# Linear attention and a sine-gated MLP in one kernel: the left-over token groups move into tile 1, batch 2 is held back, and one cast changes engine

## The chip, the cores and the metric

The kernel runs on one NeuronCore of a Trainium2 chip. The metric is the device time of one execution in microseconds. Three runs of the kernel before took 285.49, 285.60 and 286.18 us: the median is 285.6 us. The execution that was profiled took 285.96 us.

The engines are named as the profile names them: PE is TensorE (matmuls into PSUM), PEld its weight loads, DVE is VectorE, ACT is ScalarE, POOL is GpSimd and SP is the engine that issues most DMAs. Each works through its own queue in order; an instruction that waits holds up everything behind it on that engine.

## The reference

For q, k and v of shape (8 batches, 8 heads, 576 tokens, 64):

```python
q_s = softmax(q, over the 64 features)
k_s = softmax(k, over the 576 tokens)
kv  = einsum('bhsd,bhse->bhde', k_s, v)
x   = einsum('bhsd,bhde->bhse', q_s, kv)      # -> (4608 tokens, 512)
h   = x @ w_in                                # (4608, 2048)
g   = h + sin(alpha * h)**2 / (alpha + 1e-9)
out = g @ w_out                               # (4608, 512), float32
```

The two large products, x @ w_in and g @ w_out, are most of the arithmetic. The kernel computes in bf16 with float32 accumulation.

## The kernel before

**Tokens.** The 576 tokens of a batch are nine groups (j = 0 to 8) of 64. The MLP works on nine tiles of 512 tokens. Tile 0 is groups 0 to 7 of batch 0 and tile 1 is groups 0 to 7 of batch 1, so that the MLP can start when one batch is half prepared. The ninth groups of batches 0 and 1, 128 tokens together, are the first two groups of tile 2, which also takes six groups of batch 2. From there on the tokens run on in order. `place` (L276) says where each group's output goes.

**Attention of a batch.** q and k go through exp on ScalarE (`exp_q`, `exp_k`, `exp_half`, all at L118). v is cast to bf16 (`cast_v`, L137) beside a column of ones, so that the product k'v also gives the softmax sums. `norm_q` sums and scales q (L145 to L152). `kv_mm` (L173) makes the 64x64 products of all heads and `kv_norm` (L183, L186) scales them into block-diagonal weights `kbd`. q is transposed, on TensorE for batches 0 and 1 (L202) and by a DMA transpose from batch 2 on (L212). A matmul with `kbd` gives x transposed in PSUM, and a copy puts it into `xT`, the input of the MLP.

The ninth groups of batches 0 and 1 go a separate way: their q is loaded by two DMAs into the tile `q8` (in the profile: q), goes through exp (`exp_to`), is scaled by `norm_q8` on VectorE (L159 to L161), is transposed by four matmuls (tp, L518), copied (L519), multiplied with `kbd` by eight small matmuls (xp, L525) and copied into `xT` (L527).

**The MLP of a tile.** For each of 16 blocks of 128 hidden features (`mm_h`, L253, four matmuls with ki = 0 to 3 over the 512 input features) a bank of PSUM gets h; ScalarE takes the sine (L259); the square is taken by ScalarE (L261), GpSimd (L263) or VectorE (L265), as a string with one letter for each block says (A, P, D); VectorE combines sine and h into g (`combine`, L269), and with that frees the bank and the buffer s. There are four s buffers, so the sine of block n waits for the combine of block n - 4. `BANKS` (L237) names the pool of PSUM that each block uses; "k" is `ps_k`, which has a single buffer, shared with the kv products. `mm_o` (L273) multiplies g with w_out: 64 matmuls for a tile, in four accumulators. `evac_o` copies an accumulator (L285) and issues two output DMAs (L288).

**The order.** It is written out by hand. The scheduler is off: instructions stand on each engine as the program names them, and the framework adds only the waits. `flush(lag, 1)` puts the combine of a block behind the sine of the next. `take(os, n)` puts the next n matmuls of the o product of the previous tile between other work. Tile 0's o product runs while batch 1 is prepared (L440 to L484), tile 1's while batch 2 is (L511 to L552), tile 2's h while batch 3 is.

Loads of q, k and v go through five staging buffers (pool `stage`) and are issued by SP. Small VectorE copies into a buffer about to be loaded ("gate" copies, such as L418 and L426) hold a load back to that point of VectorE's queue. w_in and w_out are loaded from GpSimd's queue (L108, L111), w_out in five parts, the last (`load_wout(14, 16)`) in the seam between tiles 0 and 1.

Of the kernel before, what the change touches and what calls it, by code (L numbers as in the profile page):

```python
# [15 lines left out]
F32 = mybir.dt.float32  # L16
# [7 lines left out]
def kernel(  # L24
# [14 lines left out]
    nc = tc.nc  # L39
# [37 lines left out]
    def src_view(t, b):  # L77
        return t[b].rearrange("(i e) (p j) d -> (e p) i (j d)", e=2, j=J)
# [21 lines left out]
    def load_batch(b):  # L100
        load("q", q, b)
        load("k", k, b)
        load("v", v, b)
# [12 lines left out]
    def exp_to(dst, src, iis=range(2)):  # L116
        for ii in iis:
            nc.scalar.activation(dst[:, :, ii * 128:(ii + 1) * 128].rearrange("p j (x d) -> p x j d", x=2),  # L118
                                 src[:, ii::2], AX.Exp)

    def exp_q(b):
        A["qe", b] = att2.tile([128, J, 4 * D], BF16, name="qe")
        exp_to(A["qe", b], staged["q", b])
# [122 lines left out]
    def mm_h(t, ni, k0=0, k1=4):  # L246

        if ni == 0 and k0 == 0:
            G[t] = gpool.tile([128, nN, MF], BF16, name="g")
        hp = HP[t, ni] if k0 else bank(BANKS.get(t, 4 * "aabb")[ni])  # L250
        HP[t, ni] = hp
        for ki in range(k0, k1):
            nc.tensor.matmul(hp, win[:, ki, ni * 128:(ni + 1) * 128],  # L253
                             xT[:, ki, t * MF:(t + 1) * MF], start=(ki == 0), stop=(ki == 3))
        return hp
# [120 lines left out]
    for c in range(2, 4):  # L376
        xp = bank("l")
        attn_chunk(0, c, 0, 8, xp)
        DVE_CP(xT[:, c, 0:MF], xp)
    for ki in range(2):  # L380
        for ni in range(2, 4):
            mm_h(0, ni, ki, ki + 1)
    for ni in range(4):
        mm_h(0, ni, 2, 3)

    def h_slot(t, ni, sq, lag):
        hp = mm_h(t, ni, 3 if t == 0 and ni < 4 else 2 if t == 1 and ni < 1 else 0)
        lag.append((t, ni, hp, sine(t, ni, hp, sq)))

    def flush(lag, keep):  # L390
        while len(lag) > keep:
            combine(*lag.pop(0))
# [13 lines left out]
    def take(it, n=1000):  # L406
        for _ in range(n):
            if next(it, 0) == 0:
                return


    lag = []
    SQ = "PAPDPAPAPPDPAPAP"
    with ES:
        def load_q1():
            staged["q", 1] = st = stage.tile([128, 4, J, D], F32, name="st_q", tag="st")
            for ii in range(2):
                DVE_CP(st[:, ii, 0, 0:1], zero)  # L418
            for ii in range(2):
                nc.sync.dma_start(out=st[:, ii::2, 0:8].rearrange("p i j d -> p i (j d)"),  # L420
                                  in_=src_view(q, 1)[:, ii::2, 0:8 * D])

        def load_kv1():
            for n in "kv":
                staged[n, 1] = stage.tile([128, 4, J, D], F32, name=f"st_{n}", tag="st")
            DVE_CP(staged["k", 1][:, 0, 0, 0:1], zero)  # L426
            for ii in range(2):
                for n, t in (("k", k), ("v", v)):
                    nc.sync.dma_start(out=staged[n, 1][:, ii::2].rearrange("p i j d -> p i (j d)"),
                                      in_=src_view(t, 1)[:, ii::2])  # L430

        late = {6: load_q1, 8: lambda: load_wout(8, 12), 10: lambda: load_wout(12, 14), 13: load_kv1}
        for ni in range(nN):
            h_slot(0, ni, "DPPAPPAPPPAPPAPP"[ni], lag)
            flush(lag, 1)
            if ni in late:
                late[ni]()
        flush(lag, 0)

        accs = [bank(kind) for kind in "bbll"]  # L440
        os = o_quad(0, accs, [DVE_CP, ACT_CP, DVE_CP, DVE_CP])
        take(os, 46)
        for ii in range(2):
            exp_half("q", 1, ii, 8)
        norm_q(1, [GP, V], 8)
        load_wout(14, 16)
        for b in range(2):
            nc.sync.dma_start(out=q8[:, :, b], in_=src_view(q, b)[:, :, 8 * D:J * D])
        load_batch(2)

        def cast_v1(ii, eng):
            vv = vb[1].rearrange("p j (i c) -> p i j c", i=4)
            eng(vv[:, 2 * ii:2 * ii + 2, :, 0:D], staged["v", 1][:, ii::2])

        exp_half("k", 1, 0)
        cast_v1(0, ACT_CP)
        exp_half("k", 1, 1)
        q_tile(1)
        for ii in range(2):
            tp = ps_h[0].tile([128, 8, 128], BF16, name="tp", tag="a")  # L460
            q_transpose_ii(1, ii, 0, 8, tp)
            DVE_CP(A["qT", 1][:, ii, 0:8], tp)
        take(os, 4)

        def x_half(ii):
            xp = [bank("a") for _ in range(2)]
            for e in range(2):
                attn_chunk(1, 2 * ii + e, 0, 8, xp[e])
            for e in range(2):
                (ACT_CP, DVE_CP)[e](xT[:, 2 * ii + e, MF:2 * MF], xp[e])  # L470

        kv_mm(1, 0, ps_k, split=True)
        kv_norm(1, 0, 1)
        cast_v1(1, DVE_CP)
        take(os, 4)
        x_half(0)
        exp_to(A["qe", 1][:, J - 2:J], q8)
        take(os, 2)
        kv_mm(1, 1, ps_k, split=True)
        kv_norm(1, 1, 2)  # L480
        take(os, 4)
        x_half(1)
        nc.scalar.activation(zero, zero, AX.Sin)
        take(os)  # L484
        for ki in range(2):
            mm_h(1, 0, ki, ki + 1)
        norm_q8()
        load("q", q, 3)
        load("k", k, 3)

        for ni in range(nN):
            h_slot(1, ni, SQ[ni], lag)
            flush(lag, 1)
        cast_v(2, [GP_CP, GP_CP])
        flush(lag, 0)

# [12 lines left out]


    exp_q(2)  # L511
    exp_k(2)
    os = o_stream(1)
    take(os, 10)
    tp = ps_a.tile([128, 2, 2, 128], BF16, name="tp", tag="a")
    for b in range(2):
        for ii in range(2):
            nc.tensor.transpose(tp[:, ii, b], A["qe", 1][:, J - 2 + b, ii * 128:(ii + 1) * 128], identb)  # L518
    DVE_CP(A["qT", 1][:, :, J - 2:J], tp)  # L519
    take(os, 7)  # L520
    xp = ps_a.tile([128, 4, 2, P], F32, name="xp", tag="a")
    for c in range(4):
        ii, e = divmod(c, 2)
        for b in range(2):
            nc.tensor.matmul(xp[:, c, b], kbd[b][:, e, ii], A["qT", 1][:, ii, J - 2 + b, e * 64:(e + 1) * 64],  # L525
                             start=True, stop=True)
    DVE_CP(xT[:, :, 16 * P:18 * P], xp.rearrange("p c b n -> p c (b n)"))  # L527
    norm_q(2, [GP, V])
    exp_q(3)
    exp_k(3)  # L530
    q_transpose_dma(2, halves=True)
    load("v", v, 3)
    nc.scalar.activation(zero, zero, AX.Sin)
    take(os, 15)
    kv_mm(2, 0, ps_a)
# [14 lines left out]
    DVE_CP(xT[:, :, c0 + 6 * P:c0 + 9 * P].rearrange("p (h c) n -> p h c n", h=2),  # L550
           xp.rearrange("p h (c n) -> p h c n", c=2))
    take(os)  # L552
    cast_v(3, [DVE_CP, DVE_CP])
    q_transpose_dma(3)
    load_batch(4)

# [78 lines left out]
```

## Time and profile before

| what | value |
|---|---|
| median of three runs | 285.60 us (285.49 to 286.18) |
| the profiled execution | 285.96 us |
| its span, first to last instruction | 284.2 us |
| granted TensorE clock | 1.0 throughout |
| TensorE busy | 271.7 us, 96% |
| ScalarE busy | 225.1 us, 79% |
| VectorE busy | 193.0 us, 68% |
| GpSimd busy | 82.3 us, 29% |
| DMA | 45.80 MB, mean 161 GB/s |

Times inside the execution are microseconds from the first instruction. A line of the timeline gives start, length, engine, source line, operation, output and inputs, count, and in brackets how long the engine stood idle before and what ended that. A line of the waits gives who waited for whom, the sum, how often, and the longest. On this kernel 128x512 matmuls that follow each other start 0.216 us apart.

The stages: to 13.8 us batch 0 is prepared; tile 0's h runs from 13.8 to 28.3; tile 0's o product, mixed with batch 1's attention, to 46.8; tile 1's h to 60.6; tile 1's o product, mixed with batch 2's attention, to 77.0; tile 2's h to 93.3; from there on h of a tile alternates with the o product of the tile before, to the end.

### The profile page before, as it was taken

The numbers are of one execution on the slowest core, as the hardware profiler recorded it, in microseconds if no ns is written. First come the engines' busy times: TensorE is split into PE (matmuls) and PEld (weight loads), VectorE is DVE, ScalarE is ACT, GpSimd is POOL, SyncE is SP. The second block draws the span as 40 slices with busy tenths as digits, with TensorE's granted clock in tenths as the row PEclk, the third lists the DMA queues.
The fourth block names the chain that finished last, engine by engine and source line by source line (L and its number), as shares of the span: only waits on it lengthen the run. The fifth ranks groups of instructions, "written<-read, shape, count | busy, mean of one in ns | idle before, by whom it ended". The sixth has DMA issues, their size and how long they took to land.

```text
span 284.2 us, 4841 instructions
## 1 busy us (share of the span) xinstructions
PE 271.7 (96%) x1857; PEld 128.0 (45%) x1857; DVE 193.0 (68%) x287; ACT 225.1 (79%) x319; POOL 82.3 (29%) x78
## 2 busy tenths in 40 slices
PE   2899898999999999999999999999999999999995
PEld 1444354445444444444444444444444444444443
DVE  3957868989999768756785677667774555555412
ACT  4978847999479999899989998999877777777500
POOL 2979620674386650025002500341000000000000
PEclk9999999999999999999999999999999999999999
DMA  7999999951999119911991099118011111111143
GB/s 253 302 194 235 295 354 406 307 229 41 242 259 397 47 36 311 348 38 26 278 386 35 9 251 408 36 37 153 9 37 37 37 39 37 37 37 40 43 106 74
DMA packets 39127, 45.80 MB, mean 161 GB/s; under 512 B 17072, under 2 KB 22464, under 8 KB 39104
## 3 DMA queue, kind: packets, MB, share of 16 engines
q1 hardware_dynamic: 33360, 40.57, 45.9%
q0 software_dynamic: 5552, 4.79, 10.2%
q8 instruction: 14, 0.23, 0.3%
q10 hardware_dynamic: 192, 0.14, 0.2%
q14 instruction: 9, 0.07, 0.1%
HBM read 36.71 MB, written 9.44 MB: 162 GB/s over the span
## 4 chain that ended last, share of the span: by engine, by line
PE 71%; DMA 8%; ACT 7%; DVE 7%; issue 3%; POOL 3%; SPq 0%; POOLq 0%; ACTq 0%
PE hp L253 32%; PE op L273 32%; ACT s L259 4%; DMA wout<-in_moe_w_out_dram 3%; DVE g L269 2%; DMA st_v<-in_v_dram 2%; DMA win<-in_moe_w_in_dram 2%; DMA st_k<-in_k_dram 2%; PE xp L222 1%; DVE qs L150 1%; PE op L605 1%; PE lp L253 1%; POOL s L263 1%; DVE vb L137 1%; PE kvp L173 1%
## 5 line engine op out<-in xcount | busy, mean ns | idle before, releaser
L269 DVE SCALAR_TENSOR_TENSOR g<-s,inva_sb,hp 128x512 bf16<-128x512 f32 x128 | 94.3, 745 | 57.3 <-ACT s L261 53.1
L253 PE MATMUL hp<-xT,win 128*128 128x512 bf16 x512 | 128.3, 379 | 0.8 <-DMA win<-in_moe_w_in_dram 0.7
L273 PE MATMUL op<-wout,g 128*128 128x512 bf16 x496 | 124.4, 379 | 0.0
L259 ACT ACTIVATE s<-hp,alpha_sb 128x512 f32<-128x512 f32 x128 | 86.4, 683 | 24.0 <-PE hp L253 22.4
L253 PEld LDWEIGHTS <-win 128*128 128x128 bf16 x576 | 56.1, 98 | 68.3 <-issue 1.3
L273 PEld LDWEIGHTS <-g 128*128 128x128 bf16 x560 | 54.1, 98 | 62.7 <-issue 2.3
L261 ACT ACTIVATE s<-s 128x512 f32<-128x512 f32 x111 | 69.9, 630 | 3.5
L263 POOL TENSOR_TENSOR s<-s 128x512 f32<-128x512 f32 x30 | 32.4, 1095 | 22.3 <-ACT s L259 22.0
L152 POOL TENSOR_TENSOR qn<-qe,qs 128x1152 bf16<-128x1152 bf16 (+1 forms) x12 | 25.1, 2112 | 38.3 <-DVE qs L146 30.2
L285 DVE COPY o<-op 128x512 f32<-128x512 f32 (+2 forms) x33 | 22.1, 669 | 9.7 <-PE op L273 7.4
L137 POOL CAST vb<-st_v 128x1152 bf16<-128x1152 f32 x10 | 11.3, 1164 | 44.3 <-DMA st_v<-in_v_dram 44.3
L118 ACT ACTIVATE ke<-st_k 128x1152 bf16<-128x1152 f32 x16 | 17.9, 1151 | 3.8 <-DMA st_k<-in_k_dram 3.8
L118 ACT ACTIVATE qe<-st_q 128x1152 bf16<-128x1152 f32 (+1 forms) x16 | 17.5, 1129 | 2.5 <-DMA st_q<-in_q_dram 2.3
L145 DVE TENSOR_REDUCE qs<-qe 128x36 f32<-128x2304 bf16 x5 | 12.8, 2554 | 7.9 <-ACT qe L118 7.9
L225 DVE CAST xT<-xp 128x512 bf16<-128x512 f32 (+1 forms) x18 | 13.5, 750 | 0.0
L118 ACT ACT_TABLE_LOAD x7 | 9.0, 1283 | 1.3 <-PEq L619 1.2
L273 PE MATMUL lp<-wout,g 128*128 128x512 bf16 x32 | 8.9, 379 | 0.9 <-DVE g L269 0.9
L273 PE MATMUL hp<-wout,g 128*128 128x512 bf16 x32 | 8.9, 379 | 0.7 <-DMA wout<-in_moe_w_out_dram 0.7
L150 DVE TENSOR_REDUCE qs<-qe 128x16 f32<-128x1024 bf16 (+1 forms) x6 | 7.5, 1244 | 1.8 <-ACT qe L118 1.6
L222 PE MATMUL xp<-qT,kbd 128*128 128x256 bf16 (+1 forms) x40 | 8.2, 286 | 0.5 <-DVE xT L225 0.5
L173 PEld LDWEIGHTS <-ke 64*64 64x64 bf16 x576 | 5.8, 106 | 4.6 <-issue 1.6
L186 DVE TENSOR_TENSOR kbd<-kvp,kvr 64x256 bf16<-64x256 f32 (+1 forms) x20 | 7.4, 369 | 0.5
(83 smaller groups left out, 138.1 us busy)
## 6 DMA issues: line engine op xcount, KB each, us to landing
out_dram<-o SPq DMA_DIRECT2D x70, 128.0 KB, 2.4
st_q<-in_q_dram SPq DMA_DIRECT2D x6, 1152.0 KB, 6.4
st_k<-in_k_dram SPq DMA_DIRECT2D x6, 1152.0 KB, 9.0
st_v<-in_v_dram SPq DMA_DIRECT2D x6, 1152.0 KB, 11.3
st_k<-in_k_dram SPq DMA_DIRECT2D x4, 576.0 KB, 6.4
st_q<-in_q_dram SPq DMA_DIRECT2D x4, 512.0 KB, 6.0
st_v<-in_v_dram SPq DMA_DIRECT2D x3, 576.0 KB, 7.0
wout<-in_moe_w_out_dram POOLq DMA_DIRECT2D x3, 512.0 KB, 10.3
```

The lines of the kernel that those rows point to most:

```text
L118: nc.scalar.activation(dst[:, :, ii * 128:(ii + 1) * 128].rearrange("p j (x d) -> p x j d", x=2), src[:, ii::2], AX.Exp)
L137: engs[ii](vv[:, 2 * ii:2 * ii + 2, :, 0:D], staged["v", b][:, ii::2])
L145: nc.vector.tensor_reduce(qs, A["qe", b].rearrange("p j (i d) -> p j i d", i=4), axis=AXL.X, op=ALU.add)
L152: engs[ii % len(engs)].tensor_tensor(qn[:, ii, 0:j1].rearrange("p j (x d) -> p j x d", x=2), qe[:, ii], part.unsqueeze(3).to_broadcast([12 ...
L225: eng(xT[:, 2 * ii:2 * ii + 2, c0:c0 + n], xp[:, :, 0:n])
L253: nc.tensor.matmul(hp, win[:, ki, ni * 128:(ni + 1) * 128], xT[:, ki, t * MF:(t + 1) * MF], start=(ki == 0), stop=(ki == 3))
L259: nc.scalar.activation(s, hp, AX.Sin, scale=alpha_sb[:, ni:ni + 1])
L261: nc.scalar.activation(s, s, AX.Square)
L263: nc.gpsimd.tensor_tensor(s, s, s, op=ALU.mult)
L269: nc.vector.scalar_tensor_tensor(G[t][:, ni], in0=s, scalar=inva_sb[:, ni:ni + 1], in1=hp, op0=ALU.mult, op1=ALU.add)
L273: nc.tensor.matmul(acc, G[t][:, ni, j * 128:(j + 1) * 128], wout[:, ni, :], start=(ni == 0), stop=(ni == nN - 1))
L285: eng(o[:, cols], acc)
```

## The change

1. *Tile 0's first blocks.* The second of two xT copies moves from VectorE to ScalarE. Before, blocks 0 to 3 got their ki = 2 matmuls together and then each its ki = 3; now each block gets ki = 2 and 3 together. Of the squares, that of block 9 moves from GpSimd to ScalarE and that of block 15 from GpSimd to VectorE.
2. *The seam between tiles 0 and 1.* The loads of q8 and of batch 2 stand later in the program, and two one-element copies into q8 on VectorE hold the first of them back until VectorE has copied both halves of batch 1's transposed q. Since SP works in order, batch 2's loads follow. The exp of q8 is named a little later (its place in ScalarE's queue stays the same).
3. *The ninth groups.* Their transposes, matmuls and two copies move from tile 1's o product into tile 1's h: the transposes behind block 9, the xp matmuls behind block 12. They use `ps_k` instead of a pool that exists only later. The square of block 3 of tile 1 moves from VectorE to GpSimd.
4. *Batch 3's v.* It is loaded before the first output writes of tile 1 and before batch 2's DMA transposes, instead of behind them, and is cast by GpSimd ahead of the normalisation of batch 3's q, instead of by VectorE after tile 1's o product.

```diff
     for c in range(2, 4):
         xp = bank("l")
         attn_chunk(0, c, 0, 8, xp)
-        DVE_CP(xT[:, c, 0:MF], xp)
+        (DVE_CP, ACT_CP)[c - 2](xT[:, c, 0:MF], xp)
     for ki in range(2):
         for ni in range(2, 4):
             mm_h(0, ni, ki, ki + 1)
-    for ni in range(4):
-        mm_h(0, ni, 2, 3)
 
     def h_slot(t, ni, sq, lag):
-        hp = mm_h(t, ni, 3 if t == 0 and ni < 4 else 2 if t == 1 and ni < 1 else 0)
+        hp = mm_h(t, ni, 2 if ni < (4, 1, 0)[min(t, 2)] else 0)
...
-    SQ = "PAPDPAPAPPDPAPAP"
+    SQ = "PAPPPAPAPPDPAPAP"
...
-            h_slot(0, ni, "DPPAPPAPPPAPPAPP"[ni], lag)
+            h_slot(0, ni, "DPPAPPAPPAAPPAPD"[ni], lag)
...
         load_wout(14, 16)
-        for b in range(2):
-            nc.sync.dma_start(out=q8[:, :, b], in_=src_view(q, b)[:, :, 8 * D:J * D])
-        load_batch(2)
...
             DVE_CP(A["qT", 1][:, ii, 0:8], tp)
+        for b in range(2):
+            DVE_CP(q8[:, 0, b, 0:1], zero)
+        for b in range(2):
+            nc.sync.dma_start(out=q8[:, :, b], in_=src_view(q, b)[:, :, 8 * D:J * D])
+        load_batch(2)
         take(os, 4)
...
         x_half(0)
-        exp_to(A["qe", 1][:, J - 2:J], q8)
         take(os, 2)
         kv_mm(1, 1, ps_k, split=True)
         kv_norm(1, 1, 2)
+        exp_to(A["qe", 1][:, J - 2:J], q8)
...
+        def late_q8(ni):
+            if ni == 9:
+                A["tp8"] = tp = ps_k.tile([128, 2, 2, 128], BF16, name="tp", tag="a")
+                for b in range(2):
+                    for ii in range(2):
+                        nc.tensor.transpose(tp[:, ii, b], A["qe", 1][:, J - 2 + b, ii * 128:(ii + 1) * 128], identb)
+                DVE_CP(A["qT", 1][:, :, J - 2:J], tp)
+            elif ni == 12:
+                xp = ps_k.tile([128, 4, 2, P], F32, name="xp", tag="a")
+                for c in range(4):
+                    ii, e = divmod(c, 2)
+                    for b in range(2):
+                        nc.tensor.matmul(xp[:, c, b], kbd[b][:, e, ii],
+                                         A["qT", 1][:, ii, J - 2 + b, e * 64:(e + 1) * 64], start=True, stop=True)
+                DVE_CP(xT[:, :, 16 * P:18 * P], xp.rearrange("p c b n -> p c (b n)"))
+
         for ni in range(nN):
             h_slot(1, ni, SQ[ni], lag)
             flush(lag, 1)
+            late_q8(ni)
...
     exp_q(2)
+    load("v", v, 3)
     exp_k(2)
     os = o_stream(1)
-    take(os, 10)
...
-    take(os, 7)
...
+    take(os, 17)
     norm_q(2, [GP, V])
     exp_q(3)
     exp_k(3)
+    cast_v(3, [GP_CP, GP_CP])
     q_transpose_dma(2, halves=True)
-    load("v", v, 3)
...
     take(os)
-    cast_v(3, [DVE_CP, DVE_CP])
     q_transpose_dma(3)
```

More of the change, by code (lines that the diff above doesn't have):

```diff
@@ L511 @@
     exp_q(2)
+    load("v", v, 3)
     exp_k(2)
     os = o_stream(1)
-    take(os, 10)
[L515 to L519, printed above, removed]
-    take(os, 7)
[L521 to L527, printed above, removed]
+    take(os, 17)
     norm_q(2, [GP, V])
```

## The prediction

> **What bounds the kernel now.** I read the busy shares first, then TensorE's own waits, then the timeline around each wait, engine by engine.
>
> ```profile
> PE 271.7 (96%) x1857; PEld 128.0 (45%) x1857; DVE 193.0 (68%) x287; ACT 225.1 (79%) x319; POOL 82.3 (29%) x78
> ...
> PE lp L273 <- DVE g L269: 0.9, 1, 0.9
> PE hp L273 <- DMA wout<-in_moe_w_out_dram: 0.7, 1, 0.7
> PE hp L253 <- DMA win<-in_moe_w_in_dram: 0.7, 1, 0.7
> PE xp L222 <- DVE xT L225: 0.5, 1, 0.5
> ...
> PE hp L253 <- DVE g L269: 0.2, 1, 0.2
> ```
>
> TensorE is the bound. From the first block of h (13.80) to the end it has only a handful of waits, so a change that adds no matmul can win little and lose much. Starts are a better measure than idle, because matmul ends are modelled: eight 128x512 matmuls take 8 x 0.216 = 1.73 us, so from 28.26 the next should start at 29.99, and it starts at 31.03: 1.04 us lost. Likewise 0.81 at 44.66 (kv_mm, from 43.44, normally takes 0.41), 0.66 at 89.09, 0.33 at 103.56, and 0.29 at 74.20, where no releaser is named (it is the second half of the DMA transposes). In all 3.13 us can be won.
>
> ```profile
> 26.37 1.05 POOL L263 TENSOR_TENSOR s<-s 128x512 f32<-128x512 f32 x1
> ...
> 27.46 1.41 DVE L269 SCALAR_TENSOR_TENSOR g<-s,inva_sb,hp 128x512 bf16<-128x512 f32 x2 [1.07 <-POOL s L263]
> ...
> 28.30 0.69 ACT L259 ACTIVATE s<-lp,alpha_sb 128x512 f32<-128x512 f32 x1 [1.06 <-DVE g L269]
> ...
> 30.23 0.75 DVE L269 SCALAR_TENSOR_TENSOR g<-s,inva_sb,lp 128x512 bf16<-128x512 f32 x1 [0.24 <-POOL s L263]
> ...
> 31.03 1.89 PE L273 MATMUL lp<-wout,g 128*128 128x512 bf16 x8 [0.88 <-DVE g L269]
> ```
>
> This is the first wait: block 9's square stands on POOL behind a w_out issue (0.81 us), its combine is late, sine 13 needs that s buffer, and block 12's combine frees TensorE's bank at 30.98.
>
> **Part 1, tile 0.** Block 0 now gets its ki = 2 and 3 matmuls (16.02, 16.24) before block 1 does; before, ki = 3 of block 0 was the ninth matmul after 15.16 (16.89) and the first sine came 0.41 later (17.30). So the first sine starts at 16.65, if xT's fourth chunk is there by 16.24: it moves to ScalarE, where it stands behind the Sin load, which ends at 15.45, plus a copy of 0.60: 16.05. Square 9 goes to ScalarE (sine-to-square 0.72, square-to-sine 0.54, sine-to-sine 0.57, so +0.69 for it). Laid out with these and POOL's 1.00 per square: combine 8 ends 25.67, sine 13 needs combine 9 (26.34) and starts unhindered at 26.93, POOL issues w_out at 24.85 to 26.42, square 12 ends 28.55, combine 12 ends 29.33. TensorE wants that bank at 29.99. The wait goes: -1.04. Square 15 on VectorE (0.69) is covered by the o matmuls, which need block 15 only after 38.
>
> **Part 2, the seam.** The q8 loads and batch 2 now wait on SP behind two small VectorE copies that stand after the qT copies; w_out's last part (POOL queue) no longer shares the DMA engines with them.
>
> ```profile
> 39.23 1.06 PE L202 MATMUL tp<-identb,qn 128*128 128x128 bf16 x16
> ...
> 39.87 1.29 DVE L462 COPY qT<-tp 128x1024 bf16<-128x1024 bf16 x2 [1.99 <-PE tp L202]
> ...
> 43.87 0.72 ACT L118 ACTIVATE qe<-q 128x256 bf16<-128x256 f32 x2 [0.39 <-DMA q<-in_q_dram]
> ...
> 44.66 1.02 PE L273 MATMUL hp<-wout,g 128*128 128x512 bf16 x4 [0.73 <-DMA wout<-in_moe_w_out_dram]
> ...
> 48.21 0.67 ACT L259 ACTIVATE s<-kvp,alpha_sb 128x512 f32<-128x512 f32 x1
> ...
> out_dram<-o SPq DMA_DIRECT2D x70, 128.0 KB, 2.4
> ...
> DMA to landing us min/median/max: 10.2/10.3/10.3
> ```
>
> w_out: issued some 1 us earlier (its normalisation on POOL is), 7.9 us from issue to landing even under load, so by about 43.4 at worst and nearer 41.5; TensorE wants it at 43.85 - 1.04 = 42.81. I take -0.81. TensorE would start h(1,0) at 46.81 - 1.85 = 44.96 and needs ScalarE's xT chunk for its ki = 2 at 45.39.
>
> Added wait: ScalarE's exp of q8 (and behind it the o copy, that xT chunk, the Sin load and every sine of tile 1) waits for q8. The gate opens at 41.16 - 1.04 + 0.21 (two copies, the pair at L418 took 0.21) = 40.33; SP issues twice at 0.47, the second from 40.85. No row shows this load on a free queue: at best it lands as a 128 KB output write does, 2.4 us after issue (43.25), at worst after 10.3 us, as before behind k and v of batch 1 and beside w_out. Those have landed by then, so I take 43.25. Then exp 0.72, o copy 0.48, xT copy 0.61: 45.06, in time for 45.39; Sin load and the small activation 1.40: first sine at 46.46, against 48.21 before. Batch 2 itself (first needed at 63.29) lands some 6 us later at most than before (last at 52.4), q3 and k3 with it: hidden. Behind the waiting issues on SP stand also tile 0's eight output writes (from 46.00), whose buffers are wanted again only at 64.50.
>
> **Part 3, the ninth groups inside tile 1.** This is the step that costs. The four transposes follow h(1,9) and write the one buffer of ps_k, last held by block 7. So TensorE must stand until combine 7 has read it.
>
> ```profile
> 52.85 1.03 PE L253 MATMUL kvp<-xT,win 128*128 128x512 bf16 x4
> ...
> 55.44 1.89 PE L253 MATMUL lp<-xT,win 128*128 128x512 bf16 x8
> ...
> 55.93 0.74 DVE L269 SCALAR_TENSOR_TENSOR g<-s,inva_sb,kvp 128x512 bf16<-128x512 f32 x1
> ...
> 62.78 0.39 PE L518 MATMUL tp<-identb,qe 128*128 128x128 bf16 x4
> ```
>
> Even in the times of before, block 10 starts at 55.44 and combine 7 ends at 56.67: 1.23 us. In the changed kernel squares 2, 3 and 4 all go to POOL. From the first sine S: sine 2 ends at S + 2.52, three squares end at S + 5.65, combines 4 to 7 follow at 0.66 and the last ends at S + 8.40 (before: 56.67 - 48.21 = 8.46, the same). 46.46 + 8.40 = 54.86. TensorE has finished h(1,9) at 44.96 + 10 x 0.864 = 53.60. Wait: 1.26 to 1.30; I take 1.30. Nearest bound below: sine 7 as soon as TensorE delivers, then 0.72 + 0.63 + combine 0.75: 0.6. Above: with every square at the 1.30 of a disturbed one (52.13): 2.1. Tile 0 and the seam won 1.85; 0.55 is left. The transposes (0.23) and the xp matmuls (0.23) only change place. xp after h(1,12) waits for the qT copy, which VectorE does 2 us earlier: nothing. D square 3 leaves VectorE (0.68), two copies (0.42, 0.68) come: covered, since the first o block needs combine 10, due 1.5 us before it.
>
> A rule against this part is in the Trainium skill, "SBUF - State Buffer", section "Who interferes with whom": a GpSimd operation and a VectorE operation with two SBUF inputs exclude each other for their whole length. Rows agree in direction: POOL squares of 1.30 and 1.56 stand beside VectorE squares and casts, 1.04 elsewhere. By that rule norm_q8's product (1.51) could hold square 2 back, and the time would be 0.5 us above that of the sum below.
>
> **Part 4, after tile 1.** The VectorE queue ahead of q normalisation is shorter by the copies (0.42 + 0.60), the transposes are issued about 0.7 us earlier, TensorE comes 0.55 earlier. But v3 (1152 KB, 6.3 us from issue to landing) is now issued ahead of them, on the same SP queue, when GpSimd has cast v2 (65.31). Between -0.29 (wait gone) and +0.35 (transposes as late as before less TensorE's lead, and some); I take 0, the middle. GpSimd's cast (2.27 for two, as at 63.04) starts when v3 lands (about 71.6) and ends near 74, before its next work at 75.66.
>
> ```profile
> 78.96 3.05 DVE L137 CAST vb<-st_v 128x1152 bf16<-128x1152 f32 x2 [0.41 <-DMA st_v<-in_v_dram]
> ...
> 79.84 4.07 POOL L263 TENSOR_TENSOR s<-s 128x512 f32<-128x512 f32 x3
> ...
> 89.09 0.43 PE L222 MATMUL xp<-qT,kbd 128*128 128x320 bf16 x2 [0.49 <-DVE xT L225]
> ```
>
> Without its casts VectorE starts combining at 80.9 instead of 81.93, and POOL's squares take 1.04 again instead of 1.56. The xT copy that TensorE waited for (88.35 to 89.03) comes about 1 us earlier: -0.5 of the 0.66 (ends: 0 and 0.66). At 103.56 ScalarE was 0.7 behind TensorE when tile 2 ended; part of that goes: -0.1 (ends 0 and -0.33).
>
> **Sum.** -1.85 + 1.30 + 0 - 0.5 - 0.1 = -1.15. The profiled execution took 285.96 (span 284.2 and 1.76 around it), so 284.81; it lies 0.36 above the median of 285.6, so the median should be 284.45. A measurement of this kernel can tell about 0.3% (0.86 us) from no change.
>
> **Rivals.**
> - *Likeliest, 0.50:* as summed, 283.8 to 285.2.
> - *The wait for combine 7 is at its floor (0.6), 0.15:* 283.75. For it: ScalarE and VectorE were in step with TensorE by 57. Against: three POOL squares in a row.
> - *Tile 0 wins nothing, 0.18:* k1 and v1 are issued 1.6 us earlier (after combine 12), next to w_out's third part, which TensorE needs at 35.2 and which landed at 34.28 before; if that is late by a microsecond, or the bank is, the gate and all behind it come 1.04 later, and 285.5 is the time: no change.
> - *Slower, 0.17:* q8 lands late. Every microsecond past 43.25 delays first sine and combine 7 alike; TensorE's xT chunk is late only past 43.58. From 44.4 on the gain is gone, and if the second load takes 5 us instead of 2.4 (k1, v1 or w_out still on the engines) it lands at 45.85, and the time is 284.45 + 2.6 = 287.05. For it: q8's lines are 256-byte pieces and took 10.3 before; against: the queue ahead of it is empty.
>
> **How the numbers follow.** Faster: 0.75 of the likeliest and all of the floor case, 0.53. Same: the rest of the likeliest above 284.74 and the tile 0 case, 0.29. Slower: 0.18 with rounding. The range from 283.4 to 286.6 takes in the floor case and all but the worse half of the late q8.
>
> **What would show it.** TensorE's waits: no wait on g at 31 and none on w_out at 43; a new one, at the tp matmuls, on g, of 1.3 us near 54; no wait on xT at 88. ScalarE's wait at q8's exp about as long as 0.8, ended by the q8 DMA at 43.3. Wrong if that DMA ends past 44.4, if the tp wait is below 0.6 or above 2, or if a wait on qT's transposes at 73 exceeds 0.5.

## The result, and the profile after

The changed kernel takes 288.64 us (median of five runs, 288.44 to 289.5) against 285.60 (285.48 to 286.18): a ratio of 1.0108, 95% interval 1.009 to 1.0127. It is slower by about 1%, where 284.45 was forecast (range 283.4 to 286.6). Run again beside the kernel before, on chip 10 and on chip 12, the ratio was 1.0068 (1.0043 to 1.0092) and 1.0104 (1.0068 to 1.0139). The profiled execution took 288.47 us, with a span of 286.66 (before: 284.18).

The busy shares on the page of the changed kernel:

```profile
PE 270.4 (94%) x1828; PEld 128.3 (45%) x1857; DVE 189.4 (66%) x286; ACT 226.3 (79%) x321; POOL 81.9 (29%) x79
```

TensorE is still the bound and does the same work (of its 1857 matmuls 29 records are missing from this trace), so the 2.5 us must lie in its waits. TensorE's waits (who for whom, sum, how often, longest):

```profile
PE kvp L173 <- DVE vb L448: 1.3, 1, 1.3
PE hp L230 <- DMA qT<-qn: 1.2, 1, 1.2
PE tp L496 <- DVE g L269: 1.1, 1, 1.1
...
PE hp L273 <- DMA wout<-in_moe_w_out_dram: 0.4, 1, 0.4
```

The waits for g at 31, for w_out at 44.66 and for xT at 89 are gone, as forecast. Four others stand there instead, of which the forecast had one (tp). The timeline around the first of them, several engines in the order of time:

```profile
30.10 1.89 PE L273 MATMUL lp<-wout,g 128*128 128x512 bf16 x8
...
31.18 0.46 SPq L427 DMA_DIRECT2D st_v<-in_v_dram  x1
...
35.85 0.59 PE L273 MATMUL hp<-wout,g 128*128 128x512 bf16 x2 [0.41 <-DMA wout<-in_moe_w_out_dram]
...
42.55 0.59 PE L273 MATMUL lp<-wout,g 128*128 128x512 bf16 x2
...
43.50 0.76 DVE L448 CAST vb<-st_v 128x1152 bf16<-128x1152 f32 x1 [1.44 <-DMA st_v<-in_v_dram]
...
44.41 0.48 PE L173 MATMUL kvp<-vb,ke 64*64 64x65 bf16 x36 [1.26 <-DVE vb L448]
...
44.49 0.72 ACT L118 ACTIVATE qe<-q 128x256 bf16<-128x256 f32 x2 [1.36 <-DMA q<-in_q_dram]
```

TensorE is 0.93 us ahead at 30.10 and comes to the kv products early. But v's second half, issued at 31.18 (before: 32.51), landed at 43.48 (before: 41.65): earlier out, later in. VectorE's cast waits for it, and TensorE for the cast. In the kernel before neither waited there:

```profile
42.45 0.77 DVE L453 CAST vb<-st_v 128x1152 bf16<-128x1152 f32 x1
...
43.44 0.48 PE L173 MATMUL kvp<-vb,ke 64*64 64x65 bf16 x36
```

The later two waits of the changed kernel:

```profile
56.23 0.74 DVE L269 SCALAR_TENSOR_TENSOR g<-s,inva_sb,kvp 128x512 bf16<-128x512 f32 x1
...
57.02 0.38 PE L496 MATMUL tp<-identb,qe 128*128 128x128 bf16 x4 [1.12 <-DVE g L269]
...
67.28 0.37 SPq L97 DMA_DIRECT2D st_v<-in_v_dram  x1
...
70.90 4.19 SPq L212 DMA_TRANSPOSE qT<-qn  x2
...
76.11 0.32 PE L230 MATMUL hp<-qT,kbd 128*128 128x384 bf16 x1 [1.22 <-DMA qT<-qn]
```

The transposes stand behind combine 7 (the kvp line), as forecast. The first half of batch 2's q has landed transposed at 76.06, 3.4 us later than before (72.65), although its DMA transpose was issued only 1.2 us later (before: 69.68).

Starts of TensorE's matmuls cut the span into five stages, and this table carries most of what follows. S1 ends where tile 0's accumulators in lp start (L273), S2 at tile 1's h (L253), S3 at batch 2's kv products (L173), S4 at tile 2's h, S5 at the end of the span.

| kernel (profiled execution) | S1 | S2 | S3 | S4 | S5 |
|---|---|---|---|---|---|
| before | 31.03 | 15.78 | 21.27 | 8.93 | 207.17 |
| changed | 30.10 | 17.01 | 22.55 | 10.25 | 206.75 |
| difference | -0.93 | +1.23 | +1.28 | +1.32 | -0.42 |
| forecast | -1.04 | -0.81 | +1.30 | 0 | -0.60 |
| changed, chip 10 | 29.90 | 16.91 | 22.55 | 10.29 | 206.78 |
| changed, chip 12 | 30.42 | 16.18 | 22.55 | 10.19 | 206.78 |

S3 to S5 repeat to 0.1 us. S1 and S2 do not, and their sum (47.11, 46.81 and 46.60, against 46.81 before) varies by 0.5: up to tile 1 the changed kernel is level with the kernel before, where 1.85 us were to be won. Two stages were forecast well, S3 and S1; S2 and S4 carry the error: 2.04 and 1.32 us.

### The profile page after: what moved, and what is told of

Same layout as the page of the kernel before. It is cut to its first block, busy times and chain, and to the rows that moved or that the text cites. A ratio compares the mean times of both kernels' runs of the same rounds, so it can differ in the third digit from the quotient of the medians.

```text
span 286.7 us, 4818 instructions
## 1 busy us (share of the span) xinstructions
PE 270.4 (94%) x1828; PEld 128.3 (45%) x1857; DVE 189.4 (66%) x286; ACT 226.3 (79%) x321; POOL 81.9 (29%) x79
## 4 chain that ended last, share of the span: by engine, by line
PE 76%; DMA 8%; ACT 5%; DVE 4%; POOL 2%; issue 2%; SPq 1%; POOLq 0%; ACTq 0%
PE hp L253 34%; PE op L273 34%; DMA st_v<-in_v_dram 7%; POOL s L263 2%; ACT s L259 2%; PE xp L222 2%; DVE g L269 2%; DMA qT<-qn 2%; PE kvp L173 1%; PE op L609 1%; PE op L253 1%; PE lp L253 1%; DVE qs L150 1%; ACT vb L328 1%; SPq L298 1%
## 5 line engine op out<-in xcount | busy, mean ns | idle before, releaser
L253 PE MATMUL hp<-xT,win 128*128 128x512 bf16 x506 | 127.9, 379 | 0.8 <-DVE g L269 0.2
L273 PE MATMUL op<-wout,g 128*128 128x512 bf16 x478 | 121.6, 379 | 1.4 <-issue 0.6
L253 PEld LDWEIGHTS <-win 128*128 128x128 bf16 x576 | 56.2, 98 | 67.4 <-issue 1.1
L273 PEld LDWEIGHTS <-g 128*128 128x128 bf16 x560 | 54.1, 98 | 63.3 <-issue 2.5
L263 POOL TENSOR_TENSOR s<-s 128x512 f32<-128x512 f32 x29 | 29.8, 1040 | 26.6 <-ACT s L259 26.6
L137 POOL CAST vb<-st_v 128x1152 bf16<-128x1152 f32 x12 | 13.6, 1164 | 48.3 <-DMA st_v<-in_v_dram 48.3
L273 PE MATMUL hp<-wout,g 128*128 128x512 bf16 x31 | 8.7, 379 | 0.4 <-DMA wout<-in_moe_w_out_dram 0.4
L273 PE MATMUL lp<-wout,g 128*128 128x512 bf16 x30 | 8.4, 379 | 0.3 <-issue 0.2
L173 PEld LDWEIGHTS <-ke 64*64 64x64 bf16 x576 | 5.7, 106 | 5.6 <-issue 2.6
L173 PE MATMUL kvp<-vb,ke 64*64 64x65 bf16 x576 | 6.7, 194 | 1.3 <-DVE vb L448 1.3
```

The costliest lines, as they stand in the source:

```text
L137: engs[ii](vv[:, 2 * ii:2 * ii + 2, :, 0:D], staged["v", b][:, ii::2])
L173: nc.tensor.matmul(kvp[64 * x:64 * x + 64, e, ii * 65:(ii + 1) * 65], ke[r, j, h * 64:(h + 1) * 64], vt[r, j, h * 65:(h + 1) * 65], start= ...
L253: nc.tensor.matmul(hp, win[:, ki, ni * 128:(ni + 1) * 128], xT[:, ki, t * MF:(t + 1) * MF], start=(ki == 0), stop=(ki == 3))
L263: nc.gpsimd.tensor_tensor(s, s, s, op=ALU.mult)
L273: nc.tensor.matmul(acc, G[t][:, ni, j * 128:(j + 1) * 128], wout[:, ni, :], start=(ni == 0), stop=(ni == nN - 1))
```

## The experiments

Theory A: three new waits, each with a cause of its own. (1) At the seam the DMA engines are full, so what part 1 wins is spent on waiting for v. (2) The ninth groups' transposes wait for combine 7. (3) A DMA transpose that is issued while a load is on the engines stands until the load is through. The rivals are in the expectations. Ratios are against the kernel before on the same chip.

### One part undone at a time

**no_tile0** undoes part 1:

```diff
-        (DVE_CP, ACT_CP)[c - 2](xT[:, c, 0:MF], xp)
+        DVE_CP(xT[:, c, 0:MF], xp)
...
+    for ni in range(4):
+        mm_h(0, ni, 2, 3)
...
-            h_slot(0, ni, "DPPAPPAPPAAPPAPD"[ni], lag)
+            h_slot(0, ni, "DPPAPPAPPPAPPAPP"[ni], lag)
```

> The change without its part 1 (tile 0's block order, the copy on ScalarE and the two squares are as before). Theory A: part 1 starts the loads of k and v of batch 1 and the last part of w_out 1.2 us earlier, so that they collide; that delays w_out's third part (0.57 us lost near 35.8) and the second half of v (1.33 us lost near 44.4). Without part 1 the 1.04 us wait at 31 returns, and both others go: 288.64 + 1.04 - 0.57 - 1.33 = 287.8. Theory B: part 1 is a net win of 1.04 - 0.57 = 0.47 and the lateness of v comes from elsewhere: 289.1.

Measured: 287.39 us, 1.0066 (1.0045 to 1.0088). TensorE's waits:

```profile
PE tp L498 <- DVE g L269: 1.4, 1, 1.4
PE hp L230 <- DMA qT<-qn: 1.0, 1, 1.0
PE lp L273 <- DVE st_k L426: 0.9, 1, 0.9
```

The wait at 31 is back and the wait for v's cast has gone: v landed at 41.67. S2 is 15.12, and tile 1 starts at 45.96, earlier than in any of the three profiles of the changed kernel. Part 1 does not win 1.04; it moves the wait.

**no_hold** undoes part 2:

```diff
         load_wout(14, 16)
+        for b in range(2):
+            nc.sync.dma_start(out=q8[:, :, b], in_=src_view(q, b)[:, :, 8 * D:J * D])
+        load_batch(2)
...
-        for b in range(2):
-            DVE_CP(q8[:, 0, b, 0:1], zero)
...
```

> The change without its part 2 (q8 and batch 2 are loaded at once, as before). Theory A: v's lateness comes from part 1, so the kv wait near 44.4 stays at about 1.2 us and covers any wait for w_out: 288.6, no change. Theory B: holding batch 2 back is what lets w_out's last part overtake v; without it v lands near 41.7 as before, the kv wait (1.33) goes and a w_out wait of about 0.8 to 1.2 returns: 288.0 to 288.2 on TensorE's clock.

Measured: 287.71 us, 1.0085 (1.0058 to 1.0113). The wait for v's cast stays (1.36), v landed at 42.57 and w_out at 42.66. Holding batch 2 back neither made v late nor made w_out early.

**no_ninth** undoes part 3:

```diff
-            late_q8(ni)
...
-    take(os, 17)
+    take(os, 10)
...
+    take(os, 7)
...
```

> The change without its part 3 (the ninth groups are done in tile 1's o product, the square of block 3 is VectorE's). Theory A: the 1.29 us wait for combine 7 goes, all of tile 1 and the cast of v2 come as much earlier, so v3's load and the transposes move with it and the gain is whole: 287.35. Theory B: waits in series hide each other; TensorE reaches the transposed q earlier and waits longer there (1.38 becomes 2.6): 288.6.

Measured: 285.67 us, 1.0005 (0.9989 to 1.0022). S3 is 21.27 again, to the hundredth. The gain is larger than theory A had it, because S4 falls too (9.59): without the wait, GpSimd's cast of batch 2's v ends earlier, batch 3's v is issued at 64.83 instead of 67.28 and has landed at 70.83, soon after the first DMA transpose is issued (69.17). That took 4.1 us instead of 5.2. The waits are not independent, as theory A had assumed.

**no_v3** undoes part 4:

```diff
-    load("v", v, 3)
...
-    cast_v(3, [GP_CP, GP_CP])
     q_transpose_dma(2, halves=True)
+    load("v", v, 3)
...
+    cast_v(3, [DVE_CP, DVE_CP])
```

> The change without its part 4 (batch 3's v is loaded behind batch 2's transposes and cast by VectorE). Theory A: v3's load on SP's queue ahead of the transposes delays them by 2.2 us (they land at 76.06, 5.2 us after issue, against 3.0 before); without it they land near 73.9, TensorE arrives at 74.7, the 1.38 us goes and the 0.5 us wait at the xT copy in tile 2 returns: 287.7. Theory B: the transposes are late because VectorE's chain before them is 1.2 us late, from part 3: the wait stays, and the one in tile 2 comes on top: 289.1.

Measured: 286.46 us, 1.0033 (1.0013 to 1.0052). What names the transposed q (tile qT), the DMA transposes first:

```profile
L212 SPq DMA_TRANSPOSE qT<-qn x2: 1288/1478/1667, 71.6 to 73.4; - x2
...
DMA to landing us min/median/max: 2.8/2.9/3.0
```

The same view of the changed kernel:

```profile
L212 SPq DMA_TRANSPOSE qT<-qn x2: 1381/2044/2707, 70.9 to 72.4; - x2
...
DMA to landing us min/median/max: 4.7/4.9/5.2
```

Without the load ahead of them the transposes take 3.0 us, TensorE does not wait for them, and S4 is 8.69. The wait for xT returns only in part (S5 207.03).

### What starts each wait

**after_again** is the changed kernel once more, beside the next three.

> The changed kernel unaltered, so that it stands beside the others on one chip. 288.4 to 288.9, with the waits for v (about 1.3 to 1.5), for combine 7 (1.1) and for the transposed q (1.2) in its profile. If the wait for w_out's third part near 35.8 (0.41 in the first profile, none in the three runs that keep part 1) is not there, it belongs to one execution and not to the change.

Measured: 287.64 us, 1.0068 (1.0043 to 1.0092). The same three waits (1.73, 1.12, 1.29). The fourth, for w_out's third part at 35.85, is missing, so it belongs to single executions.

**late_tp** moves the ninth groups by two blocks:

```diff
-            if ni == 9:
+            if ni == 11:
...
-            elif ni == 12:
+            elif ni == 14:
```

> The changed kernel with the ninth groups' transposes behind block 11 and their products behind block 14 instead of 9 and 12: two blocks (1.73 us) later, when combine 7 has long read the buffer. Theory A: the 1.1 us wait at the transposes goes and nothing takes its place; the wait for batch 2's transposed q stays about 1.2, because v2's cast, v3's load and the transposes all move together: 287.4. Theory B: the gain of the run without part 3 (3.0 us) came from this wait alone and from what it delays: 285.7. Theory C: combine 11 or the two copies on VectorE make a new wait: 288.6.

Measured: 286.40 us, 1.0007 (0.9985 to 1.003). From its timeline:

```profile
57.02 0.39 PE L496 MATMUL tp<-identb,qe 128*128 128x128 bf16 x4
57.24 2.75 PE L253 MATMUL hp<-xT,win 128*128 128x512 bf16 x12
60.15 0.39 PE L503 MATMUL xp<-qT,kbd 128*128 128x64 bf16 x8 [0.16 <-DVE qT L497]
```

The transposes start at once. S3 is 21.58, 0.97 less, and the kernel 1.24 us less than the changed one on this chip. Most of what part 3 costs is its place; 0.31 above the 21.27 of before remains.

**v3_gpsimd_queue** issues batch 3's v from GpSimd:

```diff
-    load("v", v, 3)
+    load("v", v, 3, eng=nc.gpsimd)
```

> The changed kernel with batch 3's v loaded from GpSimd's queue instead of SP's, at the same moment (behind the cast of v2). Theory A: the transposes wait because they stand behind v3's packets in SP's own rings; from another queue they get their turn, land about 3.2 us after issue and the wait of 1.2 goes: 287.4. Theory B: it is the sharing of the DMA engines, whatever the queue; the transposes land 5 us after issue as now: 288.5.

Measured: 287.70 us, 1.0066 (1.0039 to 1.0092). The DMA transposes, by their tile:

```profile
DMA to landing us min/median/max: 4.6/4.9/5.2
```

As slow from another queue, so it is not the order on SP's queue. Nor is it the two output writes that are issued between the load and the transposes: in this run they had landed by 69.36, before the first transpose was issued (70.24). The Trainium skill, "DMA: Bandwidth & Descriptors", section "Issuing engines are not separate DMA queues", says that DMAs run on the same 16 engines and interleave whoever issues them; this run agrees.

**only_tile0** is the kernel before with part 1 alone (the reverse of no_tile0's edit, made in the kernel before).

> The kernel before with part 1 alone. Theory A: the wait at 31 goes (1.04), but k and v of batch 1 and w_out's last part still land when the DMA engines have carried them, near 43 to 43.5, so TensorE waits at the seam instead, about 1.3 for v or for w_out in place of 0.8: the gain left is about 0.5, 285.0. Theory B: the gain is whole: 284.4. Theory C: k and v issued earlier than w_out's third part cost more than they bring: 286.0.

Measured: 285.72 us, 0.9989 (0.9971 to 1.0007): no change. From its timeline:

```profile
30.19 1.89 PE L273 MATMUL lp<-wout,g 128*128 128x512 bf16 x8
...
43.33 0.76 DVE L451 CAST vb<-st_v 128x1152 bf16<-128x1152 f32 x1 [1.50 <-DMA st_v<-in_v_dram]
...
44.24 0.48 PE L173 MATMUL kvp<-vb,ke 64*64 64x65 bf16 x36 [1.31 <-DVE vb L451]
```

Won at 30, spent at 44: v landed at 43.31, and tile 1 starts at 46.94 (before: 46.81).

### Taking the waits away together

**early_v2** frees the staging buffer for batch 3's v sooner: GpSimd casts one half of batch 2's v behind block 9 of tile 1 and the other behind block 11.

```diff
...
+            if ni in (9, 11):
+                cast_v2((ni - 9) // 2)
...
-        cast_v(2, [GP_CP, GP_CP])
```

> The changed kernel, with GpSimd's two casts of batch 2's v put behind blocks 9 and 11 of tile 1 instead of after block 15. Their staging buffer comes free some 5 us earlier, so batch 3's v is issued near 61 to 62 and has landed (some 6 us later) near 68, before the DMA transposes of q are issued at about 70.6. Theory A (a DMA transpose that is issued while a load is still on the DMA engines stands until the load is through): the transposes take about 3.0 us again, TensorE's wait at 75 to 76 (1.2 to 1.4) goes, and the time is 287.64 - 1.3 = 286.3. The load may still be waited on if it starts late; then 286.8. Theory B (the transposes are late because GpSimd's cast of v stands ahead of GpSimd's half of the normalisation, or for another reason that has nothing to do with the load): 5 us for the transposes and 287.6 again. The waits at 44 and at 57 stay, by both.

Measured: 286.77 us, 1.0057 (1.0037 to 1.0078). Its SP timeline, then the DMA transposes by their tile:

```profile
62.83 0.37 SPq L97 DMA_DIRECT2D st_v<-in_v_dram  x1
...
71.61 3.29 SPq L212 DMA_TRANSPOSE qT<-qn  x2
```

```profile
DMA to landing us min/median/max: 2.9/3.1/3.3
```

Theory A on the cause: v landed at 68.24, the transposes take 3.3 us, TensorE does not wait, and S4 is 8.93 as before. The gain in time is less than the 1.3 expected: the changed kernel did not run on this chip, and the ratio is 0.0011 below after_again's, some 0.3 us. The profiled execution, 287.84 and the slowest of four, waited 2.40 us for batch 1's v (landed at 44.20).

**best** is early_v2 with late_tp's edit.

> The run before, with the ninth groups' transposes behind block 11 and their products behind block 14. Theory A (the three waits are independent and add): the waits on combine 7 and on the transposed q are both gone, only the wait for v's cast near 44 is left, and the time is 286.3 - 1.2 = 285.1, or 0.5 to 0.8 below the kernel before. Theory B (each win is taken back by the next wait behind it, ScalarE or VectorE being the real bound of this stretch): 286.0 to 286.4, with a new wait on g or on xT between 57 and 90.

Measured: 285.93 us, 1.0025 (1.0011 to 1.0038), 0.8 us more than theory A had it. Both waits are gone and S4 is 8.63, but S3 is 22.44, hardly less than in the changed kernel. GpSimd's two casts inside tile 1 cost what the place of the transposes had given (late_tp: 21.58).

**best_gate_k** and **best_gate_v** hold w_out's last part on GpSimd until the first half of batch 1's k, or v, has landed (the line for k; for v, "v" stands in place of "k"):

```diff
+        GP_CP(singles.tile([128, 1], F32, name="held2"), staged["k", 1][:, 0, 0, 0:1])
         load_wout(14, 16)
```

> The run before, and w_out's last part held on GpSimd until the first half of batch 1's k has landed (about 36.7, some 1 us later than it is issued in the changed kernel). Theory A (v lands late because w_out's last part shares the DMA engines with it): v's second half lands 0.3 to 0.8 us earlier and the wait at 44 shrinks by that, w_out lands near 44 and is just in time: 284.6 to 285.0. Theory B (k, v and q fill the engines by themselves, w_out's order does not matter to v): v lands where it did, and the time is that of the run before, or up to 0.5 above it if w_out is now late.

> As the run before, but w_out's last part is held until the first half of batch 1's v has landed (about 39 to 40). Theory A: v is through by 41.5, the wait on its cast is gone; but w_out's part now starts to move only near 42 to 43, lands near 46, and TensorE waits for it instead (some 2 us near 45): 286 or more. The seam then has the wait on one side or the other, because what has to land there fills the engines until 43. Theory B (the engines are not full there, only v was slow): w_out lands by 44.5 and the time is 284.

Measured: best_gate_k 285.42 us, 0.9999 (0.9986 to 1.0012). v landed at 41.64 instead of 42.54, w_out at 42.79 in time, and TensorE's wait for v's cast fell from 1.18 to 0.17. S2 is 15.35. Its timeline shows what is left in S3:

```profile
56.49 1.63 POOL L510 CAST vb<-st_v 128x1152 bf16<-128x1152 f32 x1
58.08 1.03 POOL L263 TENSOR_TENSOR s<-s 128x512 f32<-128x512 f32 x1
59.06 1.16 POOL L510 CAST vb<-st_v 128x1152 bf16<-128x1152 f32 x1
60.18 2.03 POOL L263 TENSOR_TENSOR s<-s 128x512 f32<-128x512 f32 x2
...
63.97 3.84 PE L273 MATMUL op<-wout,g 128*128 128x512 bf16 x17 [0.27 <-DVE g L269]
```

The squares of blocks 11, 13 and 15 stand behind the casts, and the o product waits for the last combines.

best_gate_v: 286.60 us, 1.0044 (1.0029 to 1.006). Neither theory. v landed at 41.24 and w_out at 42.62, both in time, but the second q8 load at 46.10. From its timeline:

```profile
46.20 0.72 ACT L118 ACTIVATE qe<-q 128x256 bf16<-128x256 f32 x2 [3.95 <-DVE o L285]
...
47.93 0.59 PE L253 MATMUL kvp<-xT,win 128*128 128x512 bf16 x2 [2.44 <-ACT xT L471]
```

ScalarE's exp comes as soon as q8 has landed (the releaser named had long been done), and TensorE's xT chunk stands behind it. So in this execution the wait went to the third of the transfers that share this stretch. At 289.34 us it is the slowest of six, 2.7 above their median, so how much of it stands in the others is not shown.

### On one chip, and what is left

**changed_same_chip**, **gate_k_only** (the changed kernel with best_gate_k's line alone) and **gate_k_early** (with early_v2's edit too) are a ladder on one chip.

> The changed kernel, unaltered, on the chip on which the next three run, so that their prices can be read as differences on one chip. 1.007 to 1.011 of the kernel before, as before: 287.5 to 288.5, by every theory.

> The changed kernel with w_out's last part held on GpSimd until the first half of batch 1's k has landed, and nothing else. Theory A (v's late landing is worth what TensorE waits for it): the wait near 44 goes, h(1,0) starts near 45.3, the first sine moves from 48.4 to about 46.9, and the wait on combine 7 stays at about 1.2 because it is counted from the first sine; 1.2 to 1.4 below the changed kernel. Theory B (TensorE's win is taken back at once, because combine 7 is bound by something that did not move): the wait on combine 7 grows to 2.4 and the time does not move by more than 0.4.

> The run before, and batch 2's v cast by GpSimd behind blocks 9 and 11 of tile 1, so that batch 3's v has landed before the DMA transposes are issued. Theory A (the transposes' wait is worth what TensorE stood there): TensorE's wait on the transposed q, 1.3, goes and the time is 1.0 to 1.3 below the run before. Theory B (the casts inside tile 1 hold up GpSimd's squares, and late combines of blocks 12 to 15 take half of it): 0.4 to 0.7 below, with waits on g near 63 to 66.

Measured: 288.79, 288.36 and 286.40 us; 1.0104 (1.0068 to 1.0139), 1.0074 (1.0044 to 1.0103) and 1.0009 (0.9991 to 1.0028). The hold on w_out did not help here: a load's landing is reported in 16 pieces, and 14 of v's landed by 41.36 instead of 42.15, but the last only at 43.29 (42.97), and the wait for the cast was 1.42 (1.00). In gate_k_early, with the same hold, v landed at 43.01 and the wait was 0.27. So what the hold gives in one execution it does not give in another; whether the chip makes the difference, and why the last pieces lag, is open. The transposes' step is worth 1.96 us in medians; the two profiles are 1.43 apart, of which 0.9 is S4 (10.07 to 9.16) and the rest lies in S1 to S3, where the landing of v varies.

**gate_k_d11x** goes from gate_k_early to theory A's end: late transposes, products behind tile 1's last combine, and block 11's square on VectorE. **d11x** is the same without the hold on w_out, and **d11x_no_tile0** is d11x without part 1.

```diff
-            if ni == 9:
+            if ni == 11:
...
-            elif ni == 12:
+            elif ni == 16:
...
-            h_slot(1, ni, SQ[ni], lag)
+            h_slot(1, ni, "PAPPPAPAPPDDAPAP"[ni], lag)
...
         flush(lag, 0)
+        late_q8(16)
```

> The run before, with the ninth groups' transposes behind block 11 and their products behind the last combine of tile 1, and the square of block 11 on VectorE instead of GpSimd. Theory A (what was left in the like kernel without the two last edits, 0.8 us of waits on g near 63 and 64 and 0.2 on the transposed ninth groups near 59, comes from GpSimd's cast standing ahead of square 11): all waits of tile 1 and its o product below 0.2, and 1.6 to 2.0 below the run before: 0.5 to 1.0 below the kernel before. Theory B (ScalarE's sines are the bound of tile 1, so that late combines stay): 1.2 below the run before, level with the kernel before, with the waits near 63 still 0.5 or more.

> The changed kernel with three edits and no hold on w_out: batch 2's v cast by GpSimd behind blocks 9 and 11 of tile 1, the ninth groups' transposes behind block 11 and their products behind the last combine of tile 1, the square of block 11 on VectorE. Only the wait for v's cast near 44 is left (1.0 to 2.2, by when v lands). Theory A (the seam's landing of v decides what part 1 is worth): level with the kernel before, -0.3 to +0.5 us. Theory B (the seam is of no weight once the later waits are gone): 0.8 us or more below the kernel before.

> The run before without part 1 of the change: the copy of xT, the order of the first matmuls and tile 0's squares as in the kernel before. Theory A: the wait of 0.9 on g at 31 is back, v lands near 41.7 and the wait near 44 is gone; the time is within 0.4 us of the run before, since TensorE reaches tile 1 at the same time. Theory B (part 1's 1.04 arrives when nothing later takes it back): 0.8 to 1.0 us above the run before.

Measured: gate_k_d11x 286.91 us, 1.0019 (0.9993 to 1.0045), with single runs from 284.85 to 289.6: inconclusive for the size. d11x 285.62, 1.0011 (0.9991 to 1.0032), and d11x_no_tile0 285.36, 1.0009 (0.9992 to 1.0025): the same with part 1 and without. That is theory A's time, though the profiled execution of d11x_no_tile0, 287.09, was late from the start (waits for w_in at 15 and 23) and shows v at 44.20 with a wait of 0.33, not v at 41.7. In d11x S3 is 22.04: square 11 on VectorE and the later place of the products together gave 0.4 against best, and 0.77 above the 21.27 of before remains, in a wait for the ninth groups' copy and one for the last combines (0.35 and 0.42 from start to start):

```profile
60.41 0.39 PE L503 MATMUL xp<-qT,kbd 128*128 128x64 bf16 x8 [0.19 <-DVE qT L497]
61.06 7.07 PE L273 MATMUL op<-wout,g 128*128 128x512 bf16 x31 [0.26 <-DVE g L269]
```

No version is measurably faster than the kernel before. The best of them are level with it.

## Why the prediction was wrong

**Part 1, right in its place and worth nothing.** The wait at 31 went and lp started at 30.10 (29.99 wanted). The rival "tile 0 wins nothing" named the direction, k1 and v1 issued earlier beside w_out; the late one was mainly v, and w_out's third part only in single executions (0.41 here). Three pairs of runs, with part 1 and without, agree that it wins nothing: the kernel before and only_tile0, no_tile0 and the changed kernel, d11x_no_tile0 and d11x.

**Part 2 is the first step that failed: "I take -0.81. TensorE would start h(1,0) at 46.81 - 1.85 = 44.96".** It asked when w_out lands (43.05 measured, within the "about 43.4 at worst") and what TensorE needs after it, but not what stands directly ahead of it: the kv products, which need v. In the kernel before these started at 43.44 without a wait, v had landed at 41.65, and the cast between takes 0.77: the slack was at most 1.02, and part 1 uses up all of it even if v lands no later. S2 came out +1.23 instead of -0.81: 1.33 for v, 0.57 for w_out's third part and 0.14 in small gaps, less the 0.81. The premise of the hold, that w_out's last part would land earlier without q8 and batch 2 on the engines, did not show either (42.66 in no_hold, 43.05 with the hold).

That part 1 makes v late is shown by no_tile0 and only_tile0; how it does so is not. In the kernel before the mean DMA share was 1.19 from 22 to 31 us, 1.16 to 36 and 1.09 to 41, which speaks for engines without idle time, where an earlier issue gains nothing. But ten of v's 16 pieces landed by 40.45 (before: 40.24), and only the other six came late, the last at 43.48 (41.65), while from 41 to 44 the share was 0.83 and the rate 172 GB/s (before: 1.11 and 345). So a few pieces lag while the engines, on average, have time to spare, and why is open. That the last part of w_out takes v's share is argued: best_gate_k supports it, gate_k_only does not.

**q8** landed at 44.38, not 43.25: at the mark from which the slower rival had the gain gone. It cost nothing, since TensorE was waiting for v; the first sine came at 48.39 instead of 46.46, because the o copy ahead of it waited for TensorE (45.90). The slower rival's mechanism did occur once, in best_gate_v (46.10, TensorE waiting 2.44 for xT).

**Part 3, right in mechanism and, with some luck, in size.** From first sine to the end of combine 7: 8.58 us (8.40 forecast), and the first sine came 1.28 after TensorE's h(1,0) (1.50 forecast). The two errors cancel: the wait costs 1.29 from start to start (1.30 forecast). It does not depend on how early TensorE or the first sine comes, as long as both move together: 8.42 to 8.58 in all profiles but the two in which the granted clock fell. The port rule priced there (0.5 for norm_q8's product holding square 2 back) was not put to the test: the sine ahead of square 2 ended at 50.96, after the product (50.80), and the square took its usual 1.04.

**Part 4 is the second step that failed: "I take 0, the middle", between -0.29 and +0.35.** It measured +1.38 from start to start at 76.11. The upper bound let the transposes land as late as before, and so with the 3.0 us that they took there, where no load was in flight. Issued at 70.90, 3.8 us before TensorE was ready for them (74.72), they would have been in time with 3.0; the first took 5.2. The sign that the forecast named for this, a wait of over 0.5 on the transposes, came (1.22). The forecast said itself that v3 is issued ahead of them and lands about 71.6, yet priced the two together at no cost. GpSimd's cast ended at 75.71, not near 74, and GpSimd then waited for the same transposes itself. The xT wait fell by 0.5, as forecast; the 0.1 at tile 3 did not come.

**Sum.** Forecast -1.15, measured +2.48 in the span. S2 (+2.04) and S4 (+1.32) make 3.36 of the 3.63 between them.

## What to carry to other kernels

Where several transfers have to land by one deadline, a wait removed ahead of it can come back at the first transfer still needed: list all of them with the landing of their last piece, not only the one that the profile names as the wait. A transfer's price taken from an idle stretch (here the transposes' 3.0 us) does not hold once another load is in flight at its issue. And a matmul slipped into a stream that runs ahead of its consumers should stand where its buffer is already free: two blocks later S3 was 0.3 us above that of the kernel before, against 1.3.

## What the runs showed that was not expected

**A DMA transpose nearly stands still until the transfers ahead of it have landed.** The packet records of the changed kernel show 256-byte packets of the transpose from 72.7 us on, while 2304-byte packets of batch 3's v run until 73; single transpose packets then took up to 1802 ns, against 18 normally, and 28 packets started between 74.0 and 74.5, where some 560 did in each half microsecond from 75.0 on. The load had landed at 73.32, but the second of the output writes issued behind it landed only at 75.17. In all nine profiles with this load in flight the full rate began at most 0.3 us before the last transfer issued ahead had landed: in late_tp at 73.1 and the write at 73.31, in no_ninth at 72.2 and the write at 72.28, and in v3_gpsimd_queue, where the writes had landed early, near 74.3 and the load at 74.37. SP's issue of the second transpose ended at nearly the same moments (75.08, 73.44, 72.48, 74.41). Which of these holds up which is open.

From issue to landing the first transpose took 5.2 us where v landed 2.4 us after its issue, 5.2 with 4.1 (the GpSimd queue), 4.8 with 1.8 (late_tp), 4.1 with 1.7 (no_ninth), and 2.9 to 3.4 where no load was in flight.

**The granted clock can fall after a wait of 2 us.** TensorE's windows of gate_k_d11x, after a wait of 2.16 us that ended at 45.26 (busy us and instructions, granted clock, DMA share, GB/s):

```profile
44.00:46.00 2.00, 0.74 (x38) 1.00 1.01 367
46.00:48.00 2.00, 2.00 (x7) 0.55 1.02 401
48.00:50.00 2.00, 2.00 (x7) 0.59 1.05 396
50.00:52.00 2.00, 2.00 (x11) 1.00 1.08 377
```

Seven matmuls in 2 us instead of ten or eleven, for about 4 us; best_gate_v shows the same (0.60 and 0.55) after its 2.44. After 2.40 in early_v2 and 2.56 in no_v3 the clock stayed at 1.00. The Trainium skill, "TensorE: Matmul & The Clock Gate", section "What's actually happening", has the clock halve after an idle window of about 3.4 us, in windows that run freely; here the clock fell after shorter waits twice and did not fall twice. That the wait is the cause, and whether its place within such a window decides, was not tried.
